# Drains of GpSimd between indirect scatters in a fused attention and mixture-of-experts kernel

## The chip, the cores and the metric

The kernel runs on one core of a Trainium2 chip. The metric is the device time of one execution in microseconds (us). The profile names the engines: PE is TensorE's matmuls, PEld its weight loads, DVE is VectorE, ACT ScalarE, POOL GpSimd, SP SyncE; a "q" behind a name means the engine's sequencer. SyncE issues most loads. GpSimd issues all scatters that go by row numbers.

## The reference, cut to what matters

Two blocks follow each other: a linear attention with a product feature map, and a mixture of experts with one expert per token.

```python
def phi(x):                                   # r = 8, so 64 features
    a, b = S1 @ x, S2 @ x
    return outer(a, b)                        # per token and head
q_p, k_p = phi(q), phi(k)                     # q, k, v: (4, 4, 1088, 32)
kv = einsum('bhsf,bhsd->bhfd', k_p, v); z = k_p.sum(axis=2)
x = (q_p @ kv) / (q_p @ z + 1e-6)             # as (B*S, H*D) = (4352, 128)

logits = x @ w_gate; e = argmax(logits, 1)    # 8 experts
gate = softmax(logits)[e]; eom = sigmoid(x @ w_output_gate)
out[rows of e] = gate * eom[:, e] * (relu(x[rows of e] @ w1[e]) @ w2[e])
```

`w1` is (8, 128, 1024) and `w2` (8, 1024, 128), all in float32.

## The kernel before

The 4352 tokens are 34 chunks of 128. A plan written out by hand (`PLAN`, words such as `kb3` or `tx0`) sets the order in which the stages are emitted, and each engine runs its instructions in that order.

*Attention.* For groups of four chunks: the sketch of k and q (`sketch`, L347), their products (`product`, L363), sums over tokens (`sums`, L406), transposes (`turned`, L417), and `attend` (L431), whose output is divided through into a row buffer x (L449; ScalarE's part is `counts`, L437) and gives the gates' logits.

*Routing.* The groups form five routes of 8, 8, 8, 4 and 6 chunks. For each route VectorE and ScalarE find each token's expert and its slot in that expert's own region of a DRAM tensor `xs`. Then `send` (L543 to L545) lets GpSimd complete the rows (token number and gate factor stand in two columns behind the 128 values) and scatter them, one indirect DMA of 128 rows of 576 bytes per chunk. All of a route's scatters stand in a row. A `pad` scatter (L812) behind the last route marks unused slots.

*Expert tiles.* The rows of an expert are read back in tiles of 128 (`rows`, L645, into `xin`). A tile is transposed (`tx`, L819, copied by `tv`, L824), multiplied by w1 (`tu`, L831), passed through Relu (`th`, L838), multiplied by w2 (`td`, L845), scaled (`ty`, L854) and scattered to its tokens' rows of the output (`to`, L859), again one indirect DMA of GpSimd per tile. There are three weight buffers, 20 of xin and 14 of y. The first 9 tiles need only the rows of the first two routes, the first NE = 17 only those of the first three; later ones wait for all rows and for the pad.

The loop runs over NS - 1 = 33 tiles; how many more there are is known only on the chip, so the rest stands in nested branches (`rest`, L890), and 37 tiles run with these inputs. GpSimd's instructions in order are thus: set-up, five routes of scatters, the pad, 37 result scatters. The program closes with a drain and a barrier of all engines (L934).

Of the kernel before, what the change touches and what calls it, by code (L numbers as in the profile page):

```python
# [51 lines left out]
def kernel(  # L52
# [12 lines left out]
    nc = tc.nc  # L65
# [47 lines left out]
    def apart(group, ins, *others):  # L113

        for g in (group,) + others:
            tc.declare_no_dep(ins.ins, group=g, reason="the rows are distinct")
        tc.add_to_no_dep_group(group, ins.ins)
# [115 lines left out]
    NE = NES[-1]  # L233
# [86 lines left out]
    def spin(n):  # L320
        ps = ps_w("ps_idle")
        for i in range(n):
            nc.tensor.matmul(ps[:, 0, :128], idle, idle, start=True, stop=True)  # L323
# [215 lines left out]
    def send(i, ey, sloti, co):  # L539
        n = len(routes[i])  # L540
        x = xts.pop(i)
        nc.gpsimd.tensor_copy(x.bitcast(I32)[:, :n, DM + 1], ids[:, routes[i][0]:routes[i][-1] + 1])
        nc.gpsimd.tensor_mul(x[:, :n, DM], co[:, :n], ey[:, :n, E + 1])  # L543
        for j in range(n):
            apart("rows", nc.gpsimd.indirect_dma_start(  # L545
                out=xs[:, :], out_offset=bass.IndirectOffsetOnAxis(ap=sloti[:, j:j + 1], axis=0),
                in_=x[:, j], in_offset=None, bounds_check=E * CAP - 1), *(f"early{k}" for k, m in enumerate(MARKS) if i > m))


    eti = consts.tile([128, NT], I32, tag="eti")  # L550
# [23 lines left out]
    NS = N // TS  # L574
# [82 lines left out]
    def first_part():  # L657
        upper()
        ps = turn(0)
        lower()  # L660
        spin(1)
        spread_S(0, ps)
# [123 lines left out]
    @stage  # L786
    def rd(i):
        send(i, have.pop(("rg", i)), have.pop(("rs", i)), have.pop(("rf", i)))
# [74 lines left out]
    def do(w, n):  # L863
        stages[w](n)
        did.add((w, n))

    with tc.manual_schedule():
        spin(WARM)
        first_part()
        for w, n in plan:  # L870
            do(w, n)
        def step_(t):


            for w, n in (("tx", t + 2), ("tv", t + 2), ("tu", t + 1), ("th", t + 1), ("td", t), ("ty", t), ("to", t)):
                if n < NT and (w, n) not in did:
                    do(w, n)

        for t in range(NS - 1):
            if t == NS - 6:  # L880
                extra = nc.values_load(more[0:1, :1], min_val=0, max_val=NT - NS,
                                       skip_runtime_bounds_check_because="as many tiles as the tables hold")
            step_(t)

        def rest(t):

            if t + 1 == NT:
                return step_(t)
            kept = [dict(x) for x in (have, xin)]
            with tc.If(extra > t + 1 - NS) as more_tiles:  # L890
                step_(t)
                rest(t + 1)
            for x, k in zip((have, xin), kept):
                x.clear()
                x.update(k)
            with more_tiles.Else():
                end[0] = t + 1
                for w in ("td", "ty", "to"):
                    do(w, t)
            end[0] = NT  # L900
        rest(NS - 1)
# [36 lines left out]
```

## Time and profile before

The time is 251.36 us (median of 3 runs, 250.72 to 252.03). The profiled execution has a span of 250.1 us.

| | busy us | share of the span |
|---|---|---|
| PE | 215.7 | 86% |
| PEld | 206.1 | 82% |
| POOL | 79.0 | 32% |
| ACT | 73.4 | 29% |
| DVE | 72.1 | 29% |

GpSimd's busy time is mostly scatters: 34 of rows with a mean of 990 ns and 37 of results with 970 ns. Within a route a scatter follows the one ahead after 0.30 us; results are 3.68 us apart once the tiles run evenly. A view by windows gives the busy time of each engine in a stretch of the span, the granted clock of TensorE, and what the DMA engines move. A view by line gives the shortest, median and longest instruction of that line; the sequencers' own instructions (drains, branches) are listed there and are not in the busy time. In the timeline, the bracket at the end of a line tells how long the engine sat idle ahead of the instruction, and what ended it; "issue" is time in which it waited for nothing that the profile shows, and "remote" is a wait whose end the profile can't assign.

### The profile page before, as it was taken

Reading aid. Unit: us, or ns where it says so; the run is one execution under the profiler, and the core shown is the slowest. Engines: PE = TensorE matmul, PEld = TensorE weight load, DVE = VectorE, ACT = ScalarE, POOL = GpSimd, SP = SyncE. Lnnn points to the kernel's source line nnn. Section 1 sums busy time; section 2 is a strip of 40 time slices with the busy share of each in tenths; the row PEclk is TensorE's granted clock in tenths of the full one; section 3 lists DMA queues with packets and bytes.
Section 4 is the critical chain, followed back from the end, with each engine's and each line's share of the span. In section 5 each row is a group of like instructions: output and inputs, shape, how many; then the busy total and the mean of one; then the engine's idle time right before and its main releaser. Section 6 shows DMA issues by size and latency. Waiting matters only on the chain.

```text
span 250.1 us, 6609 instructions
## 1 busy us (share of the span) xinstructions
PE 215.7 (86%) x2460; PEld 206.1 (82%) x2460; DVE 72.1 (29%) x240; ACT 73.4 (29%) x140; POOL 79.0 (32%) x133
## 2 busy tenths in 40 slices
PE   8999997297389778995599999999999999999830
PEld 7989994296289678995499999999999999999820
DVE  3458883258048874700000000000000000000000
ACT  2123340221005322420124324333333432432400
POOL 3600017405700374567431331232232133123120
PEclk9999999569759979998769999999999999999985
DMA  6657402111559245896398998999998998995110
GB/s 198 229 171 229 158 7 100 35 45 38 139 173 346 52 144 194 282 312 232 120 295 270 321 345 277 332 356 301 318 323 293 351 338 297 295 372 161 39 35 1
DMA packets 22787, 53.30 MB, mean 213 GB/s; under 512 B 3594, under 2 KB 9228, under 8 KB 22752
## 3 DMA queue, kind: packets, MB, share of 16 engines
q1 hardware_dynamic: 20176, 47.50, 57.9%
q0 software_dynamic: 2416, 5.33, 5.7%
q8 instruction: 21, 0.34, 0.6%
q14 instruction: 14, 0.11, 0.1%
q10 hardware_dynamic: 160, 0.01, 0.0%
HBM read 51.17 MB, written 5.52 MB: 227 GB/s over the span
## 4 chain that ended last, share of the span: by engine, by line
PE 68%; DMA 13%; another core or an unknown queue 6%; issue 6%; DVE 3%; ACT 1%; DVEq 0%; ACTq 0%
PE w L831 22%; PE kvz L845 21%; DMA out_dram<-y,xin 11%; PE t L347 8%; PE w L431 4%; PE kvz L406 4%; PE w L417 2%; DMA wt<-in_w_dram 2%; PE t L819 1%; PE w L323 1%; PE ps_kg L391 1%; DVE x L449 1%; PE ps_kzT L380 0%; ACT hT L838 0%
## 5 line engine op out<-in xcount | busy, mean ns | idle before, releaser
L831 PE MATMUL w<-xsT,wt 128*128 128x128 f32 x592 | 76.3, 282 | 5.1 <-issue 5.1
L845 PE MATMUL kvz<-wt,hT 128*128 128x128 f32 x592 | 75.5, 283 | 4.7 <-issue 4.4
L831 PEld LDWEIGHTS w<-xsT,wt 128*128 128x128 f32 x592 | 72.2, 198 | 5.7 <-issue 5.7
L845 PEld LDWEIGHTS kvz<-wt,hT 128*128 128x128 f32 x592 | 72.2, 199 | 5.7 <-issue 4.8
L859 POOL DMA_INDIRECT out_dram<-y,xin x37 | 35.9, 970 | 90.4 <-DMA wt<-in_w_dram 60.0
L838 ACT ACTIVATE hT<-w 128x1024 f32<-128x1024 f32 x37 | 37.8, 1023 | 65.9 <-issue 30.2
L824 DVE COPY xsT<-t 128x128 f32<-128x128 f32 x38 | 10.9, 290 | 118.8 <-PE t L819 101.3
L545 POOL DMA_INDIRECT xs<-x,sloti x34 | 33.7, 990 | 13.1 <-issue 8.8
L854 ACT ACTIVATE y<-kvz,xin 128x128 f32<-128x128 f32 x37 | 13.6, 367 | 36.3 <-PE kvz L845 26.4
L406 PE MATMUL kvz<-vt,kp 128*64 128x65 f32 (+1 forms) x288 | 13.7, 230 | 6.2 <-issue 6.2
L543 POOL TENSOR_TENSOR x<-co,ey 128x8 f32<-128x8 f32 (+2 forms) x5 | 1.1, 215 | 55.2 <-DVE co L536 27.6
L406 PEld LDWEIGHTS kvz<-vt,kp 128*64 128x64 f32 (+1 forms) x288 | 11.1, 140 | 8.2 <-issue 7.8
L431 PE MATMUL w<-kz,qpT 128*64 128x98 f32 x272 | 16.4, 273 | 1.3 <-issue 1.3
L431 PEld LDWEIGHTS w<-kz,qpT 128*64 128x64 f32 x272 | 14.3, 155 | 2.0 <-issue 1.7
L363 DVE TENSOR_TENSOR qp<-t,b_sb 128x1024 f32<-128x1024 f32 (+1 forms) x9 | 10.4, 1158 | 12.1 <-ACT b_sb L355 12.1
L355 ACT COPY b_sb<-t 128x128 f32<-128x128 f32 (+1 forms) x18 | 4.7, 259 | 30.1 <-PE t L347 23.9
L347 PE MATMUL t<-Sb,kT 128*64 128x64 f32 x272 | 12.4, 263 | 0.3 <-DVE Sb L331 0.3
L347 PEld LDWEIGHTS t<-Sb,kT 128*64 128x64 f32 x272 | 11.5, 175 | 1.0 <-DVE Sb L331 0.4
L363 DVE TENSOR_TENSOR kp<-t,b_sb 128x1024 f32<-128x1024 f32 (+1 forms) x9 | 10.4, 1158 | 3.8 <-ACT b_sb L355 2.0
L347 PE MATMUL t<-Sb,qT 128*64 128x64 f32 x272 | 11.5, 246 | 0.0
L423 ACT COPY qpT<-w 128x1024 f32<-128x1024 f32 (+1 forms) x9 | 8.7, 964 | 9.0 <-PE w L417 9.0
L819 PE MATMUL t<-ident,xin 128*128 128x128 f32 x38 | 10.8, 288 | 0.1
(133 smaller groups left out, 125.2 us busy)
## 6 DMA issues: line engine op xcount, KB each, us to landing
wt<-in_w_dram SPq DMA_DIRECT2D x79, 512.0 KB
xin<-xs SPq DMA_DIRECT2D x41, 72.0 KB
vt<-in_v_dram SPq DMA_DIRECT2D x8, 260.0 KB
kT<-in_k_dram SPq DMA_DIRECT2D x8, 256.0 KB
qT<-in_q_dram SPq DMA_DIRECT2D x8, 256.0 KB
out_dram<-y,xin POOLq DMA_INDIRECT x37
xs<-x,sloti POOLq DMA_INDIRECT x34
vt<-in_v_dram SPq DMA_DIRECT2D x1, 130.0 KB
```

Source lines behind the costliest of these rows:

```text
L347: nc.tensor.matmul(ps[64 * t:64 * (t + 1), j * H:(j + 1) * H], src[:, j * 128 + 64 * t:j * 128 + 64 * (t + 1)], Sb[i], start=i == 0 and j ...
L363: nc.vector.tensor_mul(res[:, :n], bview(av, [list(av.ap[1]), list(av.ap[2]), [0, r]]), bview(bv, [list(bv.ap[1]), [0, r], list(bv.ap[2])]))
L406: nc.tensor.matmul(acc[b][64 * h:64 * (h + 1), s], kp[p0:p0 + np_, j * H + 2 * s + h].rearrange("s i j -> s (i j)"), vt[p0:p0 + np_, j, s] ...
L431: nc.tensor.matmul(ps[64 * t:64 * (t + 1), 2 * j + s, :VG], qpT[:, 2 * j + s, 64 * t:64 * (t + 1)], kz[(c * 128 + 64 * t) // S][:, s], sta ...
L545: apart("rows", nc.gpsimd.indirect_dma_start(out=xs[:, :], out_offset=bass.IndirectOffsetOnAxis(ap=sloti[:, j:j + 1], axis=0), in_=x[:, j] ...
L819: nc.tensor.transpose(have["tx", t], xin[t][:, :DM], ident)
L824: nc.vector.tensor_copy(have["tv", t], have.pop(("tx", t)))
L831: nc.tensor.matmul(ps[:, c], wt[t % NW][0][:, c], xT, start=True, stop=True)
L838: nc.scalar.activation(have["th", t], have.pop(("tu", t)), ACTF.Relu)
L845: nc.tensor.matmul(ps, hT[:, c], wt[t % NW][1][:, c], start=(c == 0), stop=(c == FC - 1))
L854: nc.scalar.activation(have["ty", t], have.pop(("td", t)), ACTF.Copy, scale=xin[t][:, DM:DM + 1])
L859: apart("out", nc.gpsimd.indirect_dma_start(out=out, out_offset=bass.IndirectOffsetOnAxis(ap=x.bitcast(I32)[:, DM + 1:DM + 2], axis=0), in ...
```

## The change

GpSimd gets an instruction that holds its queue until its earlier work is done, a drain. In `send` one stands behind every second row scatter of a route. In the loop over tiles one stands behind the results of tile NE - 5 = 12, and from tile NS - 5 = 29 on behind every second tile's result, in the branches too. The purpose is to keep few scatters open at a time: rows go out in pairs, and results are settled ahead of the end. Nothing else is changed, and the computation is the same.

```diff
@@ send @@
             apart("rows", nc.gpsimd.indirect_dma_start(
                 out=xs[:, :], out_offset=bass.IndirectOffsetOnAxis(ap=sloti[:, j:j + 1], axis=0),
                 in_=x[:, j], in_offset=None, bounds_check=E * CAP - 1), *(f"early{k}" for k, m in enumerate(MARKS) if i > m))
+            if j % 2:
+
+                nc.gpsimd.drain()
@@ step_ @@
             for w, n in (("tx", t + 2), ("tv", t + 2), ("tu", t + 1), ("th", t + 1), ("td", t), ("ty", t), ("to", t)):
                 if n < NT and (w, n) not in did:
                     do(w, n)
+            if t == NE - 5 or (t >= NS - 5 and (t - NS) % 2):
+
+                nc.gpsimd.drain()
```

## The prediction

> **What bounds the kernel now.** I read the page's strips first, then the instructions of the program's closing line and of its branches, then the timeline round a run of scatters, then busy time by stage. TensorE sets the time: it is busy for 86% of the span, and from 131 us on it makes a tile every 3.68 us without a gap. So what can be won is at the end, or in the stretches where TensorE is not full.
>
> First the end. The instructions of the closing line and of the branches (engine, operation, count: shortest/median/longest ns, first and last start):
>
> ```profile
> L934 POOLq DRAIN  x3: 51/107/6034, 243.2 to 249.8; - x3
> ...
> L890 POOLq INC_SWDGE_SEM  x1: 1632/1632/1632, 241.1 to 241.1; - x1
> ...
> L931 POOLq DRAIN  x1: 182/182/182, 0.4 to 0.4; - x1
> ```
>
> GpSimd's drain behind the last scatter takes 6.03 us, from 243.2 to 249.3, with all other engines done, and the span ends at 250.1. The drain at the start, with no scatter sent, takes 0.18 us.
>
> Then the timeline, GpSimd's run of eight row scatters of the first route, and what waits beside it (start, us, engine, line):
>
> ```profile
> 36.63 1.21 POOL L545 DMA_INDIRECT xs<-x,sloti  x1 [0.70 <-POOL x L543]
> 38.15 0.98 POOL L545 DMA_INDIRECT xs<-x,sloti  x1 [0.30 <-issue]
> ...
> 40.90 0.41 PE L431 MATMUL w<-kz,qpT 128*64 128x98 f32 x5 [0.31 <-issue]
> ...
> 41.63 0.24 PE L431 MATMUL w<-kz,qpT 128*64 128x98 f32 x1 [0.31 <-issue]
> ...
> 45.82 0.97 POOL L545 DMA_INDIRECT xs<-x,sloti  x1 [0.30 <-issue]
> 46.79 0.21 POOL L542 COPY x<-ids 128x8 int32<-128x8 int32 x1
> 48.18 0.27 ACT L437 ACTIVATE rc<-w,eps 128x16 f32<-128x16 f32 x1 [11.48 <-remote]
> ```
>
> ScalarE's rc needs the attend matmuls of L431. The last of them ended at 41.87; rc starts at 48.18, 6.3 us late, and 1.4 us after the last scatter of the run. TensorE meanwhile issues four or five matmuls and pauses ("issue": no wait that the profile shows). Busy time by stage (PE, PEld, DVE, ACT, POOL, clock, DMA share, GB/s) shows the same in every long run:
>
> ```profile
> 37.00:48.00 11.00, 5.36 (x70) 3.43 (x66) 2.40 (x5) 0.00 (x0) 7.87 (x9) 0.85 0.23 78
> 48.00:58.00 10.00, 9.24 (x137) 8.85 (x138) 6.57 (x19) 3.04 (x11) 0.21 (x1) 0.66 0.10 28
> 58.00:70.00 12.00, 5.79 (x87) 4.33 (x87) 4.23 (x20) 1.28 (x2) 8.11 (x9) 0.80 0.46 135
> ...
> 98.00:107.00 9.00, 8.92 (x80) 8.73 (x79) 6.70 (x36) 3.44 (x8) 4.62 (x8) 1.00 0.86 278
> 107.00:125.00 18.00, 12.61 (x86) 11.79 (x85) 0.58 (x2) 2.60 (x4) 11.93 (x13) 0.85 0.64 219
> ...
> 150.00:237.00 87.00, 86.71 (x775) 86.33 (x774) 6.69 (x23) 33.20 (x48) 22.30 (x23) 1.00 0.86 292
> ```
>
> TensorE is half idle beside eight scatters (37 to 48, 58 to 70), loses a third beside twelve (107 to 125), nothing beside four (98 to 107), and nothing beside single scatters 3.68 us apart (150 to 237). The DMA engines are not full in the bad stages (share 0.23 and 0.46). What ties a run of scatters to TensorE's completions the profile doesn't say; that a pause between scatters prevents it, it does.
>
> **What the Trainium skill says.** "Perfetto Trace Analysis", DMA Instruction — SWDGE (GPSIMD): the profiled end of such an instruction is that of descriptor generation, not of the data. The trace agrees: 74 GB/s still flow from 47 to 48 us, after the last end at 46.79. "DMA: Bandwidth & Descriptors", Anatomy of one DMA — SWDGE (gpsimd) path: some 2.0 us of fixed cost, mostly the receipt of the write; I use it as the upper price of waiting for a landing. "TensorE: Matmul & The Clock Gate", Part 1: an array that was idle for about 3.4 us runs at half clock until it has been busy as long. The trace agrees: 0.50 from 45 to 54 us, and the stage 48 to 58 has a mean of 0.66. No page says what a drain of GpSimd waits for.
>
> **The change, part by part.** It removes and moves nothing; every other instruction stands where it stood. It adds 17 drains in send (routes of 8, 8, 8, 4, 6 chunks: 4+4+4+2+3) and 5 among the results (behind tiles 12, 29, 31, and in the branches 33, 35; 37 tiles run).
>
> *Price of one drain.* Low: 0.18 us, the drain at the start. High: a landing (2.0 us, the page) and 0.18. I take 1.5 us: the data stop about 1.3 us after a scatter's end (46.79 to 48), and 0.2. A pair then takes 2 x 1.28 + 1.5 = 4.05 us instead of 2.57, and a run of eight 16.2 instead of 10.2.
>
> *Closing drain.* If the last scatter (end 242.17) lands 1.3 us later, at 243.5, then 5.8 us of the 6.03 are something else. 72 scatters have been sent by then with no drain among them: 80 ns each, if the drain settles each of them. That is an inference; the alternative is a fixed cost. With the change one scatter, that of tile 36, is left: 0.1 to 0.3 us behind its landing. This saves 5.5 us, straight off the end. The five result drains settle what is left over beforehand: up to 17 x 0.08 + 1.3 = 2.7 us at tile 29, 1.5 at the later ones. GpSimd idles 2.71 us ahead of each result scatter (its line in the waits), and behind it is queued only the next result, which has 14 buffers of y. Hidden.
>
> *Drains in send.* Queued behind them are the next pair, the next route's copies, the pad scatter and the results. Those who wait: the loads of xin, thus the first tile transposes. Before, the first xin load is issued at 71.6, when the second route's rows have landed, and TensorE reaches the first tile only at 82.05. By then it has lost some 15 us: 5.6 idle in 37 to 48, 6.2 in 58 to 70, the rest at half clock. With the pauses I expect most of that back, so that TensorE reaches the tiles near 68 and has to wait for rows. The rows: first route from 36.6, four pairs to 52.8; second route 53.6 (58.21 before) to 69.8; landed about then; xin at 71.6 as before, and 2.8 us from issue to transpose (215.32 to 218.13 in the steady part): first tile at 74.4. Gain 7.6 us, and the bound of this stage moves from TensorE to GpSimd.
>
> *From the first tile on.* 82.05 to 250.1 is 168.05 us. Without any loss it would be 8.3 to the first tile's end, 36 x 3.68 = 132.5, 1.8 where TensorE's branch stalls (236.6 to 238.4) and 9.6 behind it: 152.2. So 15.8 us are lost, nearly all beside runs of scatters. With the change, nine pairs at perhaps 0.35 us: 3.3. But GpSimd is now later than the tiles: third route from 77.8 to 94, fourth to 103, fifth to 116.3, pad 117.6. By then (117.6 - 82.7) / 3.68, nine to ten results are waiting, and about 13 go out back to back until the drain at tile 12. Such a run of twelve (107 to 122) cost about 11.7 us before; I take 7. Loss 10.3 instead of 15.8: gain 5.5.
>
> Sum: 251.4 - 5.5 - 7.6 - 5.5 = 232.8, so 233 us.
>
> **Rivals.**
> 1. *Pauses cure everything, the late run of results too.* All 15.8 come back: 251.4 - 5.5 - 7.6 - 15.8 = 222.5. For it: four scatters in a row cost nothing. Against: the results still run without a pause.
> 2. *Pairs stall TensorE as the runs did, only the end is won.* Pauses of 1.5 us would be too short; the tiles start as before, and 251.4 - 5.5 = 246, 241 to 250 with small gains or late rows. For it: delayed completions come through only 1.2 to 1.8 us after a run.
> 3. *No effect that counts: the closing drain's cost is fixed and a drain is cheap.* About 251. Against: 0.18 us at the start with nothing sent, 6.03 at the end.
> 4. *Slower.* The drain lengthens the runs by 6.0/10.2, and the stall goes with the length: of some 30 us lost in all, 18 more, minus 5.5, and part hidden: 258 to 263. Against: single scatters, with pauses of 2.7 us, leave TensorE full.
>
> **How the numbers follow.** My forecast (227 to 241) 0.50; rival 1 (below 227) 0.17; rival 2 0.17; rival 3 0.04; rival 4 0.12. Predicted 233. The range 221 to 249.5 leaves out rival 4, rival 3 and the far edge of rival 1; it holds a drain of 0.18 us (less lateness, so towards 222) as well as one of 2.2. Faster by over 0.5%: 0.84; within: 0.04; slower: 0.12.
>
> **What would show it.** Right: the closing drain falls from 6.0 to under 2 us; drains of about 1.5 us stand behind pairs; in the stages beside them TensorE is above 0.8 busy; ScalarE's wait of 11.5 us is gone; the first tile transpose stands near 74 and waits for xin. Wrong: a closing drain that keeps its 6 us; TensorE still issuing four matmuls at a time beside pairs; a first tile later than 82; a second stall of TensorE beside the run of results behind the pad that is as long as now.

## The result and the profile after

The changed kernel takes 259.71 us (median of 4 runs) against 251.04 us before (also 4 runs): ratio 1.032, with an interval from 1.025 to 1.038. Here and below a time is the median of all runs, and a ratio is that of the runs in the chip's faster state. The kernel is slower by 8.7 us where 18 us of gain were forecast. In a later set it took 260.19 us.

The closing line, the branches and the added drains by line (engine, operation, count: shortest/median/longest ns, first and last start), after:

```profile
L940 POOLq DRAIN  x3: 46/113/1969, 254.0 to 257.0; - x3
...
L896 POOLq INC_SWDGE_SEM  x1: 207/207/207, 253.6 to 253.6; - x1
...
L550 POOLq DRAIN  x17: 3336/3375/6248, 35.4 to 127.2; - x17
...
L883 POOLq DRAIN  x5: 2704/5692/6013, 163.5 to 248.2; - x5
```

The closing drain falls from 6.03 to 1.97 us, and the branch's INC_SWDGE_SEM from 1.63 to 0.21. From the end of the last scatter to the end of the span there are now 2.7 us (254.62 to 257.3) instead of 7.9: 5.2 us won, where 5.5 were forecast. A drain in `send` (L550) has a record of 3.4 us in idle stretches and of up to 6.2 us beside weight loads. The record begins while the first scatter of the pair still runs, so it takes in the second one; what the drain adds is the pause behind it.

The timeline after, round the first route (compare the wait of 11.48 us of ScalarE's rc before):

```profile
38.74 0.27 ACT L437 ACTIVATE rc<-w,eps 128x16 f32<-128x16 f32 x1 [3.59 <-PE w L431]
...
39.85 0.97 POOL L545 DMA_INDIRECT xs<-x,sloti  x1 [2.28 <-issue]
41.12 0.97 POOL L545 DMA_INDIRECT xs<-x,sloti  x1 [0.30 <-issue]
...
43.12 1.52 PE L431 MATMUL w<-kz,qpT 128*64 128x98 f32 x31
44.68 0.27 ACT L437 ACTIVATE rc<-w,eps 128x16 f32<-128x16 f32 x1 [0.41 <-PE w L431]
44.71 0.97 POOL L545 DMA_INDIRECT xs<-x,sloti  x1 [2.61 <-issue]
```

Behind the second scatter of a pair GpSimd pauses 2.2 to 2.6 us instead of 0.30; beside the weight loads of the third route it is up to 4.95 us. TensorE now issues 31 matmuls in one go, and rc follows 0.04 us behind the last. The stall is cured, also as forecast. Busy time by stage (PE, PEld, DVE, ACT, POOL, clock, DMA share, GB/s) shows the cure in its first line, to be compared with this line of the kernel before:

```profile
37.00:53.00 16.00, 9.60 (x135) 7.61 (x132) 6.46 (x18) 1.91 (x5) 7.87 (x9) 0.74 0.19 58
```

The lines behind it show what was lost. After:

```profile
37.00:53.00 16.00, 14.04 (x282) 12.31 (x279) 12.08 (x42) 4.42 (x14) 6.44 (x8) 1.00 0.22 67
...
107.00:117.00 10.00, 6.65 (x60) 6.46 (x58) 0.29 (x1) 2.78 (x4) 4.40 (x7) 1.00 0.36 134
117.00:131.00 14.00, 0.00 (x0) 0.00 (x0) 0.00 (x0) 0.00 (x0) 6.33 (x9) 0.51 0.09 32
131.00:147.00 16.00, 10.18 (x73) 10.18 (x74) 0.87 (x3) 2.67 (x4) 8.78 (x9) 0.68 0.73 232
```

From 117 to 131 us TensorE, VectorE and ScalarE do nothing at all; only GpSimd works, at the fifth route. (Before, TensorE was busy for 12.61 of the 18 us from 107 to 125.) The timeline of that place says what all wait for:

```profile
109.80 0.27 PE L822 MATMUL t<-ident,xin 128*128 128x128 f32 x1
...
130.64 0.19 POOL L814 CAST pai<-pa 128x1 int32<-128x1 f32 x1 [1.53 <-issue]
131.41 0.98 POOL L815 DMA_INDIRECT xs<-pad,pai  x1 [0.58 <-POOL pai L814]
...
134.96 0.33 SPq L648 DMA_DIRECT2D xin<-xs  x1
...
136.82 0.47 PE L822 MATMUL t<-ident,xin 128*128 128x128 f32 x1 [23.17 <-DMA xin<-xs]
```

The first and the last line are the transposes of tiles 8 and 9; the last but one is tile 9's load. It goes out at 134.96, when the pad scatter has landed; SyncE had waited for that since 107.1. The same three lines of the kernel before:

```profile
119.23 0.42 PE L819 MATMUL t<-ident,xin 128*128 128x128 f32 x1
...
120.51 0.33 SPq L645 DMA_DIRECT2D xin<-xs  x1
...
129.11 0.42 PE L819 MATMUL t<-ident,xin 128*128 128x128 f32 x1
```

In the list of waits of SyncE's queue (us in total, times, longest), after:

```profile
SPq L648 <- DMA xs<-pad,pai: 27.8, 1, 27.8
```

and in the same list of the kernel before:

```profile
SPq L645 <- DMA xs<-pad,pai: 3.6, 1, 3.6
```

The wait was there before, 3.6 us long, and hidden. It corrects a sentence of the kernel's description above: tiles 9 to 16 need only the rows of three routes, but their loads stand behind the pad in program order and, as built, wait for it. The slack of this wait is not its 3.6 us. It is the time from when tile 9's rows are there to their transpose: before, some 122.4 to 129.11 (120.51, and 1.86 us from load to transpose as after), thus 6.7 us by this estimate. And it shrinks as TensorE is freed of stalls and comes earlier. Once it is used up, each microsecond that `send` takes longer lands on tile 9.

### The profile page after: what moved, and what is told of

It is laid out like the page before. It is cut to its first block, busy times and chain, and to the rows that moved or that the text cites. A ratio compares the mean times of both kernels' runs of the same rounds, so it can differ in the third digit from the quotient of the medians.

```text
span 257.3 us, 6631 instructions
## 1 busy us (share of the span) xinstructions
PE 204.6 (80%) x2460; PEld 197.1 (77%) x2460; DVE 71.8 (28%) x240; ACT 73.4 (29%) x140; POOL 78.9 (31%) x133
## 4 chain that ended last, share of the span: by engine, by line
PE 35%; issue 23%; DMA 19%; POOLq 9%; POOL 7%; SPq 4%; DVE 1%; ACT 0%
PE w L834 11%; PE kvz L848 11%; DMA out_dram<-y,xin 11%; POOLq L550 8%; POOL xs L545 6%; DMA xin<-xs 5%; PE t L347 4%; SPq L656 2%; PE kvz L406 2%; DMA wt<-in_w_dram 2%; PE w L431 2%; DMA xs<-pad,pai 1%; PE w L323 1%; PE w L417 1%; SPq L642 1%
## 5 line engine op out<-in xcount | busy, mean ns | idle before, releaser
L848 PE MATMUL kvz<-wt,hT 128*128 128x128 f32 x592 | 73.7, 279 | 2.0 <-SPq L896 2.0
L848 PEld LDWEIGHTS kvz<-wt,hT 128*128 128x128 f32 x592 | 70.5, 195 | 2.2 <-issue 2.2
L822 PEld LDWEIGHTS t<-ident,xin 128*128 128x128 f32 x38 | 5.7, 151 | 40.6 <-DMA xin<-xs 38.6
L431 PE MATMUL w<-kz,qpT 128*64 128x98 f32 x272 | 14.7, 257 | 0.9 <-DVE lg L457 0.4
L431 PEld LDWEIGHTS w<-kz,qpT 128*64 128x64 f32 x272 | 12.8, 141 | 2.0 <-issue 1.4
L347 PE MATMUL t<-Sb,kT 128*64 128x64 f32 x272 | 10.0, 225 | 1.4 <-DVE kp L363 0.7
L347 PE MATMUL t<-Sb,qT 128*64 128x64 f32 x272 | 10.5, 225 | 0.8 <-issue 0.8
L406 PE MATMUL kvz<-vt,kp 128*64 128x65 f32 (+1 forms) x288 | 10.6, 223 | 0.4 <-DVE kp L363 0.4
L347 PEld LDWEIGHTS t<-Sb,kT 128*64 128x64 f32 x272 | 8.9, 138 | 2.2 <-DVE kp L363 0.8
L347 PEld LDWEIGHTS t<-Sb,qT 128*64 128x64 f32 x272 | 9.1, 138 | 1.6 <-issue 1.2
```

Of the source, the lines that this page charges most:

```text
L347: nc.tensor.matmul(ps[64 * t:64 * (t + 1), j * H:(j + 1) * H], src[:, j * 128 + 64 * t:j * 128 + 64 * (t + 1)], Sb[i], start=i == 0 and j ...
L406: nc.tensor.matmul(acc[b][64 * h:64 * (h + 1), s], kp[p0:p0 + np_, j * H + 2 * s + h].rearrange("s i j -> s (i j)"), vt[p0:p0 + np_, j, s] ...
L431: nc.tensor.matmul(ps[64 * t:64 * (t + 1), 2 * j + s, :VG], qpT[:, 2 * j + s, 64 * t:64 * (t + 1)], kz[(c * 128 + 64 * t) // S][:, s], sta ...
L822: nc.tensor.transpose(have["tx", t], xin[t][:, :DM], ident)
L848: nc.tensor.matmul(ps, hT[:, c], wt[t % NW][1][:, c], start=(c == 0), stop=(c == FC - 1))
```

## The experiments

"Free" below means this edit, which lets the loads of tiles 9 to 16 wait for the last scatter of the third route instead of the pad (routes four and five and the pad are put into the group "late" where they are issued):

```diff
@@ rows @@
+        if NES[0] <= t < NE:
+            tc.declare_no_dep(ins.ins, group="late", ...)
+            tc.add_manual_dep(ins.ins, <last scatter of the third route>, ...)
```

"Tail" means result drains behind tiles 12, 29 and 31 only, without the two in the branches:

```diff
-            if t == NE - 5 or (t >= NS - 5 and (t - NS) % 2):
+            if t == NE - 5 or t in (NS - 5, NS - 3):
```

A filler is a write of GpSimd that nobody reads; it took 1.91 us each time:

```diff
+    filler = consts.tile([32, 2150], F32, tag="filler")
...
-                nc.gpsimd.drain()
+                nc.gpsimd.memset(filler, 0.0)
```

All runs, each beside the kernel before in the same set:

| run | in send | results | free | us | before | ratio [interval] |
|---|---|---|---|---|---|---|
| e1 | none | five | no | 247.42 | 250.46 | 0.990 [0.987, 0.993] |
| e2 | pairs, drain | none | no | 259.3 | 250.46 | 1.038 [1.027, 1.049] |
| e3 | two routes, drain | five | no | 244.0 | 250.46 | 0.980 [0.971, 0.989] |
| e4 | pairs, drain | five | yes | 251.35 | 250.46 | 1.005 [1.001, 1.008] |
| e5 | two routes, drain | five | yes | 238.94 | 227.19 | 1.049 [1.037, 1.060] |
| e6 | two routes, filler | five | no | 237.98 | 227.19 | 1.041 [1.031, 1.051] |
| e7 | none | tail | no | 223.29 | 227.19 | 0.979 [0.971, 0.986] |
| e8 | fours, drain | five | no | 240.38 | 227.19 | 1.052 [1.040, 1.064] |
| e9 | the change itself | five | no | 260.19 | 227.28 | 1.140 [1.134, 1.147] |
| e10 | two routes, drain | tail | yes | 237.24 | 227.28 | 1.033 [1.025, 1.042] |
| e11 | none | tail | yes | 218.44 | 227.28 | 0.958 [0.953, 0.964] |
| e12 | as e6 | five | no | 237.3 | 227.28 | 1.044 [1.039, 1.048] |
| e13 | as e6 | five | no | 243.76 | 250.33 | 0.974 [0.967, 0.982] |
| e14 | as e11 | tail | yes | 246.38 | 250.33 | 0.982 [0.975, 0.989] |
| e15 | as e10 | tail | yes | 245.6 | 250.33 | 0.982 [0.976, 0.989] |
| e16 | pairs, filler | tail | yes | 241.55 | 250.57 | 0.963 [0.956, 0.970] |
| e17 | pairs, filler | tail, fillers | yes | 233.56 | 250.57 | 0.933 [0.927, 0.938] |

The kernel before took 250 us in three of these five sets (and where it was first measured) and 227 us in the other two. How the two conditions differ is read below, at e5 to e9.

### e1 and e2: one half of the change each

```diff
e1, send:  -            if j % 2:
           -                nc.gpsimd.drain()
e2, step_: -            if t == NE - 5 or (t >= NS - 5 and (t - NS) % 2):
           -                nc.gpsimd.drain()
```

> The five drains among the results alone, none in send. Theory W (the loss of the changed kernel comes from send's drains, since they put off the pad scatter, for which the load of tile 9 waits; the result drains only settle what the closing drain would settle): everything up to 226 us as in the kernel before, closing drain about 2 us instead of 6.0, so 251.0 - 5.2 = 246 us (245 to 247.5). Rival R (a result drain holds GpSimd 5.7 to 6.0 us, and late results hold y and xin buffers, so part of the gain is given back): 248.5 us or more, with TensorE waiting somewhere behind 163 us.

> The 17 drains in send alone, none among the results. Theory W, and the closing drain settles what is unsettled since the last drain (38 scatters, at (6.03 - 1.97) / 71 = 57 ns each): closing drain about 4.1 us, so 259.7 + 2.2 + what the branch's semaphore instruction takes more (up to 1.4) = 262 to 263.5 us; TensorE idle from 113 to 137 us as in the changed kernel. Rival (a fixed cost of the closing drain that any recent drain takes away, or not a matter of the count at all): 259.7 (closing drain 2 us) or 265 (closing drain 6 us).

e1 gains 2.4 us by its ratio, about half of what the shorter closing drain is worth. The timeline of its end shows why:

```profile
234.59 0.97 POOL L859 DMA_INDIRECT out_dram<-y,xin  x1 [2.71 <-ACT y L854]
...
237.72 0.37 ACT L854 ACTIVATE y<-kvz,xin 128x128 f32<-128x128 f32 x1 [3.40 <-PE kvz L845]
240.04 0.97 POOL L859 DMA_INDIRECT out_dram<-y,xin  x1 [4.49 <-issue]
```

The last y is ready at 238.09, and its scatter starts 1.95 us later: the drain behind tile 35 (4.61 us here) holds GpSimd until 238.96, and 1.08 us more pass until the scatter. In the changed kernel that drain took 2.70 us, the last y came later behind it, and the last scatter followed y in 0.27 us. Rival R of e1 is thus half right: part of the gain is given back, but at the last scatter and not by a wait of TensorE.

e2 carries the loss alone, so the result drains are not its cause. Its closing line and branch, with 38 scatters sent since the last drain:

```profile
L937 POOLq DRAIN  x3: 46/107/3253, 256.1 to 260.0; - x3
...
L893 POOLq INC_SWDGE_SEM  x1: 952/952/952, 254.7 to 254.7; - x1
```

3253 / 38 = 86 ns each for the drain; before, with 72, it was 84 ns. INC_SWDGE_SEM took 207 ns with one scatter (the change), 952 with 38 and 1632 with 72: about 0.2 us and 20 ns for each. Both grow with the number of scatters that no drain has settled, and the rival of a fixed cost falls. The expected 4.1 us of the closing drain had put the landing of the last scatter on top; that is not added. From the end of its last scatter e2 needs 4.4 us, 1.7 more than the change. Its total is not the expected 2 to 4 us higher; the two ratios (1.038 and 1.032) differ by 1.6 us, which fits, but their intervals overlap.

### e3 and e4: is it the wait for the pad?

```diff
e3, send: -            if j % 2:
          +            if j % 2 and i < 2:
e4:       all drains as in the change, and "free"
```

> Drains in send behind the pairs of the first two routes only (8 of the 17); the result drains stay. Theory W: the first tile at 78.5 us as in the changed kernel, the third to fifth routes run without pauses, the pad lands by 121 us instead of 135, so TensorE's idle time behind tile 8 shrinks from 23.4 us to 0 to 6 us: 251.0 - 5.2 (closing drain) - 3.5 (first tile) = 242 us (238 to 246). Rival P (the pauses themselves, or the changed meeting of scatters and weight loads, cost the time, not the load of tile 9): half of the drains left, so about half of the loss, 250 us or more.

> All drains stay; the loads of tiles 9 to 16 wait for the last scatter of the third route, whose rows they need, and no longer for the pad. Theory W: the load of tile 9 goes out at 107 us when SyncE reaches it, TensorE runs on at 113 us, and the next wait for the pad is that of tile 17's load, reached about 128 us and released at 135, with two tiles of lead: 259.7 - 23.4 - 1.8 (half clock) + up to 7 = 235 to 242 us. Rival P (GpSimd is too slow with its drains, whoever waits): results come out from 136 us on anyway, buffers of y run out or the weight loads stand still, and 250 us or more remain.

e3 agrees with theory W: with drains in two routes only, the pad is scattered at 111.59 instead of 131.41, and the kernel beats the one before. (The expectation calls 78.5 us the first tile of the changed kernel; that is its second, the first stands at 73.83, in e3 at 73.90.) e4 falls between the two: it takes 7 to 8 us off the change, not 18 to 25. By stage:

```profile
117.00:131.00 14.00, 14.00 (x128) 14.00 (x127) 1.17 (x4) 5.34 (x8) 3.33 (x5) 1.00 0.95 320
...
147.00:160.00 13.00, 7.82 (x50) 7.15 (x50) 0.29 (x1) 1.39 (x2) 9.96 (x11) 0.86 0.74 230
160.00:175.00 15.00, 10.61 (x72) 10.57 (x72) 0.87 (x3) 3.26 (x6) 6.36 (x7) 0.67 0.70 225
```

The hole from 117 to 131 is filled, so the wait for the pad was its cause. But two things come in its place. The drains now stand beside full weight loads and last longer:

```profile
L554 POOLq DRAIN  x17: 3355/3779/7177, 36.0 to 140.0; - x17
```

so the pad starts at 144.22, and tile 17's load, which does need it, waits 10.0 us. And the 13 results that have piled up go out back to back from 145.5 to 161.8, beside which TensorE is idle in part, as in the kernel before (7.82 of 13 us busy): ScalarE stands idle for 8.4 us ahead of an hT of that stretch.

### e5 to e8, and e9: the same kernels under another condition

```diff
e5: as e3, and "free"          e6: as e3, fillers in place of the drains
e7: as e1, with "tail"         e9: the change, nothing edited
e8, send: -            if j % 2:
          +            if j % 4 == 3:
```

> Both edits of the two better versions: drains in send behind the pairs of the first two routes only, result drains as in the change, and the loads of tiles 9 to 16 wait for the third route alone. With drains in two routes (244.0 us) SyncE still waited for the pad at tile 9 and TensorE lost some 9 us between 108 and 128 us. Theory W (that loss is the wait for the pad): 236 to 239 us, TensorE full from 108 us on. Rival T (it is TensorE's stall beside the run of scatters from 95 to 119 us, which stand there without a pause): 242 to 244 us as without the edit, with TensorE idle in pieces beside the run.

> In the first two routes a write of 2150 elements by GpSimd (about 2 us) in place of each drain, none in the other routes, result drains as in the change. It pauses as long as a drain does but waits for no landing and settles nothing; it adds no result. Theory Q (the pause between pairs is what keeps TensorE's completions in time): TensorE as busy beside the first route as with drains (13.8 of 16 us from 37 to 53; 9.6 in the kernel before), time that of drains in two routes, 242 to 246 us. Rival L (it is the waiting for the landing, few transfers being open at a time): TensorE near 9.6 of 16 us there, and 246 to 250 us.

> The result drains alone, without the two in the branches (behind tiles 33 and 35): behind tiles 12, 29 and 31. Theory B (with the result drains alone, the drain behind tile 35 still held GpSimd when the last y was ready at 238.1 us, so that the last scatter started 1.95 us late): the last scatter follows y within 0.4 us, the closing drain settles five scatters within the landing of the last, about 2 us as with all five, ratio to before 0.982 (against 0.990 with all five). Rival (the closing part grows by 0.1 us for each of five unsettled ones and more, so nothing is won): 0.988 to 0.992.

> Drains in send behind every fourth scatter instead of every second (8 instead of 17), the result drains as in the change, tile 9's load still behind the pad. Theory W: the chain of scatters is some 9 x 2.2 to 5 = 20 to 30 us shorter where it was on the path, the pad lands about 118 us instead of 135, TensorE's wait at tile 9 shrinks from 23 us to under 6; four in a row cost TensorE little beside the first two routes: 239 to 245 us. Rival (TensorE stalls as soon as four scatters follow each other while others are still open): TensorE under 11 of 16 us from 37 to 53 us, 246 to 251 us.

> The changed kernel itself once more, since two chips gave 250.5 and 227.2 us for the kernel before. Theory C (a chip where the kernel before takes about 250 us stalls TensorE beside runs of scatters, and one where it takes about 227 does not; send's drains cost the same on both): where before is about 250 us the ratio is 1.03 again; where it is about 227 us, nothing is cured and the whole lateness of the chain is lost, 254 to 260 us, ratio 1.12 to 1.15. Rival (the difference of the chips lies elsewhere and scales all alike): ratio 1.03 on either.

In the set of e5 to e8 the kernel before took 227.19 us, so what these four were to tell about the 250 us case they can't tell. e7 shares all its instructions up to tile 12 with the kernel before. Its stage with the first two routes:

```profile
37.00:53.00 16.00, 14.68 (x322) 13.76 (x318) 14.34 (x45) 5.51 (x16) 12.37 (x15) 1.00 0.42 124
```

TensorE is 14.68 of 16 us busy beside 12 unpaused scatters; before, in this stretch, it was 9.60, and in e1 9.23. Under this condition runs of scatters don't stall TensorE, there is nothing to cure, and every kernel with pauses in `send` is slower than before. e9 agrees: the change takes 260.19 us here and 259.71 there, and its ratio is 1.14 instead of 1.03, as theory C had it. With drains it is GpSimd's chain that sets the time, and that is nearly the same under both (the pad starts at 134.37 and 131.41).

Theory C called this a property of the chip. That is not shown: e5 to e8 and e16 and e17 carry the same chip number, with 227.19 and 250.57 us before. What sets the condition stays open.

e5, e6 and e8 show what the pauses cost where there is nothing to cure: by their ratios 9 to 12 us, with the gain of the result drains already taken off. e7 transposes the first tile at 59.70 us, e9, with all drains, at 77.49. In e8 the drains are fewer. Their records are longer (5.80 us in the median) because they begin while the second scatter of four still runs; the wait behind the fourth is 1.5 us in idle stretches, as behind a pair. The pad starts at 112.73 and tile 9's load waits 14.5 us for it. e7 confirms the tail: its last scatter follows y in 0.27 us, and 5 unsettled scatters cost nothing beyond the landing of the last (closing drain 2.14 us).

### e10 to e12: freed loads

```diff
e10: two routes, "free", "tail"     e11: no drain in send, "free", "tail"
e12: e6 again
```

> Drains in send in the first two routes only, tile 9's load freed from the pad, result drains behind tiles 12, 29 and 31 only. Where before is about 250 us, theory W: 235 to 240 us (two routes alone 244.0, less the wait at tile 9, less 1.5 us at the last tile), ratio 0.94 to 0.96. Rival T (TensorE's stall beside the unpaused run from the third route on is what is left): 241 to 243. Where before is about 227 us: late first tiles, ratio 1.03 to 1.05.

> No drain in send, tile 9's load freed from the pad, result drains behind tiles 12, 29 and 31. Theory C: where before is about 250 us, TensorE's stalls beside the routes stay, the tail gains about 4 us and tile 9 up to 4 more: 242 to 246 us; where before is about 227 us, 219 to 221 us, the best there, because the 3.7 us that TensorE waited for tile 9's rows are gone. Rival (the pad's wait at tile 9 is hidden behind TensorE's stall on either chip): 246 and 223 us, as with the tail alone.

> A write of about 2 us by GpSimd in place of each drain of the first two routes, none in the other routes, result drains as in the change. Where before is about 250 us: theory Q (a pause is what TensorE's completions need) TensorE above 13 of 16 us busy from 37 to 53 us, 242 to 246 us, as with drains in two routes; rival L (the waiting for the landing does it) near 9.6 of 16 us and 246 to 250 us. Where before is about 227 us both say 236 to 239 us, as late rows cost it.

The set ran under the 227 us condition again, so e12 tells nothing new on the pause. e10, at 1.033, stands where it was expected under this condition. e11 agrees with theory C: 218.44 us, better than both kernels and 0.6 us below the expected range. In e7 the load of tile 9 still waits 8.3 us for the pad and TensorE 3.71 for the load; in e11 that wait is gone, and the ratio goes from 0.979 to 0.958.

### e13 to e15: pause or landing?

e13 is e6, e14 is e11, e15 is e10 once more, now with 250.33 us before.

> The pauses without drains in the first two routes, hoped for on a chip where the kernel before takes about 250 us. There, theory Q (a pause is what TensorE's completions need): TensorE above 13 of 16 us busy from 37 to 53 us, 242 to 246 us, as with drains in two routes; rival L (few open transfers, thus waiting for the landing, is what they need): near 9.6 of 16 us, 246 to 250 us. Where before is about 227 us: 236 to 239 us once more.

> No drain in send, tile 9's load freed from the pad, result drains behind tiles 12, 29 and 31. Where before is about 250 us: 242 to 246 us, since the stalls beside the routes stay (theory C); rival, if the freed loads alone cure the stretch behind 108 us: 238 to 241. Where before is about 227 us: 218 us again.

> Drains in send in the first two routes, tile 9's load freed, result drains behind tiles 12, 29 and 31. Where before is about 250 us: 237 us, as on the other chip, since the drains put both chips on the same path (theory C); rival T (TensorE still stalls beside the unpaused run from the third route on): 241 to 244. Where before is about 227 us: 237 again.

e13 by stage:

```profile
37.00:53.00 16.00, 13.97 (x285) 12.40 (x284) 12.15 (x43) 4.71 (x14) 14.40 (x13) 1.00 0.24 73
```

With 1.9 us fillers, which wait for no landing, TensorE is as busy as with drains (13.82 in e3), and the time is the same within the intervals. So no drain is needed for the cure, as theory Q says. It does not yet part the pause from the landing: in this idle stretch a drain ends some 1.4 us behind the end of its scatter (70.66 to 72.09 in the changed kernel), so within a filler both scatters of a pair may have landed too. e16 tells more.

e14 and e15 answer that freeing tile 9 adds nothing that shows under this condition. e14 has no pause in `send`, "free" and "tail": 246.38 us and ratio 0.982, which is what "tail" alone was expected to give ("tail" alone was not run here; e1 has 0.990). In e15 the stall of rival T is there: from 107 to 117 us TensorE is 4.07 of 10 us busy beside the unpaused scatters of the fifth route and the results. Its 245.6 us lie 8.6 above the expected 237, nearer to rival T's 241 to 244.

### e16 and e17: short pauses everywhere

```diff
e16: fillers behind every pair of all routes, "free", "tail"
e17: e16, and in to:
+        if t % 2 and t < NE - 5:
+            nc.gpsimd.memset(filler, 0.0)
```

> A write of about 2 us by GpSimd behind every pair of every route, no drain in send, tile 9's load freed from the pad, result drains behind tiles 12, 29 and 31. The written pause does not grow beside weight loads as a drain does (1.9 us against up to 6.25), so the chain of scatters should end about 127 us (131 in the changed kernel, 144 in the one with all drains and tile 9 freed). Where before is about 250 us: TensorE full from 81 to about 127 us, then some 10 results in a row that stall it: 240 to 244 us; rival (the late rows cost as much as with drains): 249 to 252. Where before is about 227 us: 238 to 245 us, the lateness alone.

> As the kernel with written pauses behind every pair of rows, and such a pause also behind every second result of the first 12 tiles. Where before is about 250 us: the run of results behind the pad stalls TensorE no more, 234 to 240 us; rival (that stall has nothing to do with the run of results): the same time as without these pauses. Where before is about 227 us: the same as without them, within 1.5 us.

By stage, e16:

```profile
107.00:117.00 10.00, 10.00 (x92) 10.00 (x92) 0.88 (x3) 3.37 (x6) 8.76 (x9) 1.00 0.92 315
117.00:131.00 14.00, 10.79 (x90) 10.09 (x89) 0.58 (x2) 2.78 (x4) 10.98 (x13) 1.00 0.88 304
131.00:147.00 16.00, 14.51 (x102) 14.35 (x102) 1.17 (x4) 5.46 (x8) 3.76 (x5) 0.79 0.71 233
```

and e17:

```profile
107.00:117.00 10.00, 10.00 (x92) 10.00 (x92) 0.88 (x3) 3.35 (x6) 8.76 (x9) 1.00 0.96 322
117.00:131.00 14.00, 13.89 (x125) 13.70 (x124) 1.17 (x4) 5.37 (x8) 12.17 (x11) 1.00 1.00 349
131.00:147.00 16.00, 16.00 (x146) 16.00 (x145) 1.17 (x4) 6.15 (x9) 14.43 (x12) 1.00 0.99 354
```

A filler keeps its 1.91 us beside weight loads, so the pad starts at 119.3 instead of e4's 144.2, and nothing waits for it. From 107 to 117 us TensorE is busy throughout, where e15, without pauses there, has 4.07 us. In e4 the drains of that stretch end 4.0 to 5.2 us behind the end of their scatters, in e16 the next pair follows after 2.1. If a landing takes as long in e16 (its profile doesn't record it), several scatters are open there at a time and TensorE is full all the same: that speaks for the pause and against the number of open transfers. In e16 nine results then go out back to back (120.6 to 131.8) and TensorE stalls beside them: 102 matmuls from 131 to 147 instead of 146. Six pauses between those results take that away, and the time falls by 8.0 us, to 233.56. Both rivals fall; e17 comes out 0.4 us below what was expected of it. Neither was run under the 227 us condition.

## Why the prediction was wrong

*Closing drain: right.* 5.5 us were forecast, 5.2 came, and "80 ns each" was 84 to 86 for the drain. The shorter INC_SWDGE_SEM, which the forecast did not count, is part of it. "Hidden" was wrong for one of the five result drains: the one behind tile 35 can delay the last scatter (1.95 us in e1).

*The stall and its cure: right, for the condition it was read under.* Pauses of about 2 us between pairs bring TensorE back to 14 of 16 us (change, e3, e13). That a pause without a drain is enough is shown; what ties the scatters to TensorE is not, and in two sets the tie was not there.

*Price of one drain: too low.* 1.5 us were taken, from one landing in an idle stretch (46.79 to 48 is 1.2 us, not 1.3, a slip that changes little). There the pitch of a pair came out at 4.5 to 4.9 us (4.05 forecast): the drain ends 1.4 to 1.8 us behind the second scatter, near what was taken, but another 0.8 pass until the next scatter. Beside weight loads it is far more, and the upper price of 2.2 us does not hold either: in the third route the drains end up to 4.3 us behind the scatter (102.67 to 106.98). Pairs start at 80.88, 86.41 and 93.19 there, so the pitch is 5.5 and 6.8 us. The pad starts at 131.41, against 117.6 in the forecast. Of these 13.8 us, 3.1 are a later start of the third route (80.88 against 77.8; GpSimd had waited 7.7 us for VectorE's co), and about 10 are the route itself, 26.1 us long instead of 16.2.

*First tile: right in time, in part by luck, and wrong in worth.* 74.4 us were forecast, 73.83 came, and it waited for rows. Drains that cost more were made up for by a first route that began 1.5 us earlier (35.07 against 36.6) and by a load that took 1.8 us to its transpose instead of 2.8. But the next loads of xin stand on SyncE among weight loads, and the transposes follow at 78.55, 82.23 and 85.89, where before they came at 83.33, 84.40 and 86.35: of the lead of 8.3 us, 0.5 is left at the fourth tile. By tile 8 TensorE, freed of stalls, has a lead of 9.4 (109.80 against 119.23).

*The clock: right in level, loose in timing.* Half clock was said to follow 3.4 us of idleness. Before, it is there from 44.7 us on, only 0.5 us after TensorE's last matmul of that stretch, which had pauses ahead, and until 54.9, 6.1 us after the work resumes at 48.76. After, it comes 3.6 us after TensorE stops (113.65 to 117.2) and goes 4.3 us after it resumes (136.82 to 141.1). No term of the sum hangs on this.

*From the first tile on: the step that failed.* It let late rows do nothing but pile up results ("nine to ten results are waiting"). It named "the loads of xin" as those who wait behind the drains, and then followed this only for the first tile; for tile 9 the wait was put at nothing. Tile 9's load waits for the end of the whole chain. TensorE is ready for it at 113.65 and starts at 136.82, 23.2 us later. With the pad at 117.6, as forecast, and the rest of the chain unchanged, it would still have waited 9.4 us, by estimate: so 9.4 of the 23.2 come from the overlooked wait alone, and 13.8 from the later pad. The lead of 9.4 us at tile 8 turns into a lag of 7.7 at tile 9 (136.82 against 129.11): 17.1 us in one wait. Another 4.7 are lost behind it, at first by half clock (5.76 us from tile 9's transpose to tile 10's). From the first tile to the last scatter's end the change takes 180.8 us (73.83 to 254.62), before 160.0 (82.16 to 242.17): 20.8 more, where 5.5 less were forecast. With 8.3 us won ahead of it and 5.2 behind, the spans differ by some 7 us, as measured (257.3 against 250.1). The forecast's sum of this part also has a slip: nine pairs at 0.35 us are 3.15 us, not 3.3.

The line that tells it, `xs<-pad,pai: 3.6`, stood in the waits of the kernel before. The reader of a profile is tempted to skip it: short and hidden. It should be read as "this load already goes out only when the pad has landed; when will its reader be there once the stalls are gone?"

*The rivals.* Rival 4 gave 258 to 263 us, and the time fell there, but by another road: TensorE's stall did not grow with the length of the runs. Rival 2 falls with the cure, rival 3 with the closing drain. e17, with short pauses for drains, tile 9 freed and the results broken up as well, is at 233.56 us, near the forecast 233; it is another kernel, and the nearness confirms no term of the sum.

## What to carry to other kernels

Before an instruction is put into a queue, list every load that waits for anything behind it, to the end of that queue, and what slack each of these waits has, from the landing of its data to their first use. A short hidden wait says nothing of that slack; it says that the releaser already sets when the load goes out. Count the slack against the schedule as it will be: where the change lets the reader come earlier, the slack shrinks by as much. If only a pause is wanted, use one of fixed length: the filler kept its 1.91 us beside weight loads, where drains grew from 3.4 to as much as 7.2 us. Drains for the sake of the end belong ahead of the last results, not directly before the last (e1 against e7).

## What the runs showed of the hardware

- The record of a GpSimd drain behind two scatters, which takes in the second of them, is 3.4 us long in idle stretches and up to 7.2 us beside weight loads (e4). At the end of the program the drain costs 84 to 86 ns for each scatter that no drain has settled (72 and 38 of them), with about 2 us for few; INC_SWDGE_SEM takes about 0.2 us and 20 ns for each.
- Runs of indirect scatters 0.30 us apart delay TensorE in some sets (9.2 to 10.6 of 16 us busy) and not in others (14.7), with the same program ahead of tile 12 and once under the same chip number. The time before was 250 and 227 us. In all profiles of the 250 us sets the list of DMA issues gives no time from issue to landing, neither for loads nor for scatters; in all of the 227 us sets it does (medians of 2.4 to 3.9 us for rows, 4.9 to 5.4 for results). What lies behind both is open.
- A pause of 1.9 us behind every second scatter is enough to prevent the delay, even beside weight loads at 322 to 354 GB/s (e17).
